# Layer 1 of the last token block as seven multiplications, and the steps around it regrouped

## The chip, the core and the metric

One core of a Trainium2 chip runs the whole kernel. Times are device microseconds (us) of one launch; the time of a kernel is the median of its runs. The engines of the core are TensorE (PE: multiplications, with PEld for the loading of the stationary operand), VectorE (DVE), ScalarE (ACT), GpSimd (POOL) and SyncE (SP, which only issues DMAs here). Each takes its own instructions in the order in which the program wrote them, and waits on semaphores for the others.

## The reference

```python
# q, k, v: (8, 8, 576, 64); a causal window of 64 positions
attn = softmax(where(0 <= rel < 64, q @ k.T / 8, -1e6)) @ v        # (8, 8, 576, 64)
x    = attn.transpose(0, 2, 1, 3).reshape(4608, 512)
h    = maximum(x @ w_in, 0.0)                                       # (4608, 2048): layer 1
out  = (h * h) @ w_out                                              # (4608, 512): layer 2, float32
```

## The kernel before

**Blocks and stages.** The 4608 tokens are nine blocks of 512: blocks 0 to 7 are the first 512 positions of the eight batches, block 8 (`B`, the last) the 64 positions left over in each. The scheduling is by hand (`tc.manual_schedule`): what is written first is issued first on each engine. From `n = 1` to `n = 8` the program goes through stages. Stage `n` lists layer 2 of block `n` (`second`) and layer 1 of block `n + 1` (`first`), merges them by the string `order` (a "1" takes the next step of layer 1, a "2" one of layer 2) into the list `fill`, and hangs everything else (attention of block `n + 2`, sums, loads) on places of that list with `put(i, ...)`. Before item `i` of `fill` the work put at `i` is issued. Stage 7 has layer 2 of block 7 and layer 1 of block 8 and no attention any more; stage 8 has layer 2 of block 8 alone, and then the kernel ends.

**Layer 1 (`F1`, L351).** For one chunk of 128 features: four multiplications of 128x128 by 128x512 into a PSUM bank (`hps`, one of two banks of `ps_f1`), then VectorE takes max(., 0) into `hr` (L361), and ScalarE squares it into `h2` in fp16 (L362). Sixteen such items make a block.

**Layer 2 (`L2S`, L453).** From block 2 on it is done with seven multiplications in place of eight (Strassen's method in Winograd's form): both matrices are cut into 2x2 parts, sums of parts are made beforehand (`S_sum` of h, per half `s` of 128 tokens, into `hsum`; `T_sum` of `w_out`, once, into `wsum`), and the products 1, 2, 6, 5, 7, 3, 4 accumulate in three places: `c` (called chain), and the two halves `pa`, `pb` of another bank (side). One item is eight multiplications of 128x128 by 128x256. Products 6, 7 and 4 go on adding to what stands in `c`, and product 3 to what stands in `pb`; after each product ScalarE (`scaled`, L460) or VectorE (`plus`, L463) takes the state that is wanted to the output tile `osb`. So 14 items make layer 2 of a block. In stage 8 the first half of the tokens uses two extra banks (`more`, from `ps_f1`), so that two halves can alternate.

**Queues.** The ten buffers of pool `stp` (tag "st") stage the loads of q, k, v; the five of `tpool` (tag "T") hold transposed q and k; the four of `apool` (tag "pm") the attention weights. `at_ps` are two PSUM tiles of two banks each, which the attention uses. x of block 8 reaches `xT` by DMA transposes (L336). Output is stored by SP; the last stores go out by SP, POOL and ACT (L490 to L509).

Of the kernel before, what the change touches and what calls it, by code (L numbers as in the profile page):

```python
# [8 lines left out]
FP32 = mybir.dt.float32  # L9
FP16 = mybir.dt.float16  # L10
AF = mybir.ActivationFunctionType
ALU = mybir.AluOpType
# [3 lines left out]
def kernel(  # L16
# [13 lines left out]
    nc = tc.nc  # L30
# [3 lines left out]
    P = 128  # L34
    HP = H // 2
    NBLK = B + 1
    DMC = DM // P
    FFC = DFF // P
# [16 lines left out]
    ps_f1 = ctx.enter_context(tc.tile_pool(name="ps_f1", bufs=2, space=bass.MemoryType.PSUM))  # L55
# [47 lines left out]
    st = {}  # L103
# [12 lines left out]
    def copy(engine, out, in_):  # L116
        if engine is nc.scalar:
            engine.activation(out=out, in_=in_, func=AF.Copy, scale=1.0)  # L118
# [126 lines left out]
    pm, av, xs, xT = {}, {}, {}, {}  # L245
    at_ps = [ps_at.tile([P, 2, 512], FP32, name=f"at{i}") for i in range(2)]
# [84 lines left out]
    def X(g, hp, engine=nc.scalar, pool=ps_tr, tag="tr", own=None):  # L331

        if g not in xT:
            xT[g] = xtpool.tile([P, DMC, 512], FP16, name="xT", tag="xT")
        if g == B:
            nc.sync.dma_start_transpose(out=xT[g][:, hp, :].rearrange("p (j t) -> p j t", j=4),  # L336
                                        in_=xs[g, hp][:].rearrange("p j h d -> p (j h d)"))
            return
        if own is not None:
            tr = at_ps[own][:, 0, :].bitcast(FP16).rearrange("p (a b) -> p a b", a=2)  # L340
        else:
            tr = pool.tile([P, 2, 512], FP16, name="xtr", tag=tag)
        for jp in range(4):
            nc.tensor.transpose(out=tr[:, 0, jp * P:(jp + 1) * P], in_=xs[g, hp][:, jp, :, :],  # L344
                                identity=ident[:])
        copy(engine, xT[g][:, hp, :], tr[:, 0, :])


    h2 = {}

    def F1(g, f, pool=ps_f1, tag="f1", into=None):  # L351
        if g not in h2:
            h2[g] = h2pool.tile([P, FFC, 512], FP16, name="h2", tag="h2")
        hps, done = open_f1.pop((g, f), (None, 0))
        if hps is None:
            hps = into if into is not None else pool.tile([P, 512], FP32, name="hps", tag=tag)
        for c in range(done, DMC):
            nc.tensor.matmul(hps[:], w_in_sb[:, c, f * P:(f + 1) * P], xT[g][:, c, :],  # L358
                             start=(c == 0), stop=(c == DMC - 1))
        hr = opool.tile([P, 512], FP32, name="hr", tag="hr")  # L360
        nc.vector.tensor_scalar(out=hr[:], in0=hps[:], scalar1=0.0, scalar2=None, op0=ALU.max)  # L361
        nc.scalar.activation(out=h2[g][:, f, :], in_=hr[:], func=AF.Square)  # L362
# [41 lines left out]
    HF = FFC // 2  # L404
    HC = DM // 2
# [12 lines left out]
    def s_of(k, s):  # L418
        return S_sb[:, k - 1, :, 128 * s:128 * s + 128]

    def minus(out, a, b, op=ALU.subtract, engine=None):
        (engine or nc.vector).tensor_tensor(out=out, in0=a, in1=b, op=op)  # L422
# [11 lines left out]
    def S_sum(g, k, s):  # L434
        if k == 1:
            minus(s_of(1, s), a_of(g, 1, 0, s), a_of(g, 1, 1, s), ALU.add)
        elif k == 2:
            minus(s_of(2, s), s_of(1, s), a_of(g, 0, 0, s))
        elif k == 3:
            minus(s_of(3, s), a_of(g, 0, 0, s), a_of(g, 1, 0, s))  # L440
        else:
            minus(s_of(4, s), a_of(g, 0, 1, s), s_of(2, s))

    def product(to, a, b, start):
        for f in range(HF):
            nc.tensor.matmul(to, a[:, f, :], b[:, f, :], start=start and f == 0, stop=f == HF - 1,  # L446
                             skip_group_check=True)

    def flush():
        while to_store:  # L450
            to_store.pop(0)()
# [59 lines left out]
    ORDER = (1, 2, 6, 5, 7, 3, 4)  # L511

    seq = list(range(NBLK))
# [3 lines left out]
    with tc.manual_schedule():  # L517
# [21 lines left out]
        dve, pool, act = nc.vector, nc.gpsimd, nc.scalar  # L539
# [60 lines left out]
        three = [in_f1, in_f1, in_f2]  # L600
# [60 lines left out]
        first = iter([lambda f=f: F1(g1, f, into=at_ps[1][:, 1, :] if f == 2 else None) for f in range(FFC)])  # L661
# [5 lines left out]
        def A(g, hp, i=1):  # L667
            AV(g, hp, i)
            N(g, hp)
# [36 lines left out]
        done = 12  # L706
        chain = ps_f2.tile([P, 512], FP32, name="chain", tag="f2")
        side = ps_tr.tile([P, 512], FP32, name="side", tag="tr")
        for n in range(1, NBLK):
            g = seq[n]  # L710
            last = n == NBLK - 1
            one = None if last else seq[n + 1]
            if n == 1:
                second = [lambda ts=ts, i=i: F2(g, ts, i, None, None, into=(chain, side)[ts % 2])
                          for ts in range(4) for i in range(4)]
            elif last:
                more = [ps_f1.tile([P, 512], FP32, name="more", tag="f1") for _ in range(2)]
                banks = [(more[0][:, 0:HC], more[1]), (chain[:, 0:HC], side)]
                second = [lambda p=p, s=s: L2S(g, p, s, banks[s])
                          for p, s in ((1, 0), (2, 0), (1, 1), (6, 0), (2, 1), (5, 0), (7, 0),  # L720
                                       (6, 1), (3, 0), (4, 0), (5, 1), (7, 1), (3, 1), (4, 1))]
            else:
                second = [lambda p=p, s=s: L2S(g, p, s, (chain[:, 0:HC], side))
                          for s in range(2) for p in ORDER]
            first = [] if last else [lambda f=f: F1(one, f) for f in range(FFC)]
            order = ("22222222" + 8 * "112" if n == 1 else
                     "2" * 14 if last else
                     ("2112121212121211" if n == 2 else "1212121212121211") + "21212121121122")
            a, b = iter(first), iter(second)
            fill = [next(a if c == "1" else b) for c in order]  # L730
            at = {}

            def put(i, *work):
                at.setdefault(i, []).extend(work)

            if n == 1:
                put(0, lambda: Sc(g2, 3), lambda: A(g2, 2))
                put(2, lambda: M(g2, 3))
                put(3, lambda: X(g2, 2, own=1))
                put(5, lambda: A(g2, 3))  # L740
                put(7, lambda: X(g2, 3, own=1))
                for i, k in ((1, 1), (3, 2), (6, 3), (8, 4)):
                    put(i, lambda k=k: T_sum(k))
            else:
                for i, k, s in (((0, 1, 1), (0, 2, 1), (2, 4, 0), (3, 3, 1), (4, 4, 1)) if last else
                                ((2, 4, 0), (4, 1, 1), (6, 2, 1), (9, 3, 1), (18, 4, 1))):
                    put(i, lambda k=k, s=s: S_sum(g, k, s))
            if not last:
                end = len(fill) - 1
                put(24 if n == 1 else 20, lambda: S_sum(one, 3, 0))  # L750
                put(end if n == 1 else end - 1, lambda: S_sum(one, 1, 0))
                put(end, lambda: S_sum(one, 2, 0))
            base = 4 * (n + 2)
            for i, two in zip((11, 22) if n == 1 else (9, 20) if n == 2 else (9, 17) if n == 6 else (8, 19),
                              (units[base:base + 2], units[base + 2:base + 4])):
                for t, u in enumerate(two):
                    if u is not None:
                        put(i, lambda u=u, t=t: Sc(*u, i=t))
                        put(i + 3 + t, lambda u=u: M(*u))
                        put(i + 6, lambda u=u, t=t: A(*u, i=t))  # L760
                        put(i + (7 if u[0] == B else 8 + t), lambda u=u, t=t: X(*u, own=t))
            for i, group in enumerate(fill):
# [38 lines left out]
```

## Time and profile before

| what | us |
|---|---|
| median of 3 runs (range) | 298.98 (298.89 to 299.31) |
| the profiled execution | 298.21 |
| its span, first to last instruction | 296.2 |
| stage 7: first matmul of layer 1 of block 8 to first of stage 8 | 253.63 to 279.67 |
| stage 8: to the start of its last matmuls' item | 279.67 to 291.02 |
| last copy of the output on ACT, last DMA issue | 292.11, 292.52 |

Read it so: times in the traces count from the start of the span, and what lies around the span (298.21 - 296.2 = 2.0 us) is launch and end. A group of matmuls in the timeline starts when its first one starts; the next group's start tells when PE was free again, since the ends shown include the way through the array. A duration on ACT or DVE is start to finish of one instruction; the next one may start a little before that end.

### The profile page before, as it was taken

To read this page: it belongs to the slowest core of one execution; us is meant where nothing else is said; L and a number is where in the kernel's file an instruction comes from. 1 tells how busy PE (TensorE), PEld (TensorE's weight loads), DVE (VectorE), ACT (ScalarE), POOL (GpSimd) and SP (SyncE) were. 2 spreads that over 40 slices of the span, in tenths; PEclk is the share of its full clock that TensorE was granted. 3 is DMA by queue.
4 is the path that set the end of the run, shared out by engine and by line. 5 is a ranking of instruction groups with operands and counts; after the bars stand their busy time and mean duration, and the time that the engine had idled before them with its cause. 6 is when DMAs were issued, how large, how long until landed. Compare 5 with 4: busy or idle time off the path is not lost.

```text
span 296.2 us, 7372 instructions
## 1 busy us (share of the span) xinstructions
PE 287.7 (97%) x2905; PEld 180.3 (61%) x2905; DVE 216.3 (73%) x379; ACT 170.3 (57%) x292; POOL 125.8 (42%) x215
## 2 busy tenths in 40 slices
PE   7899999999999999999999999999999999999994
PEld 5543545555445466667666766676667666766783
DVE  4677539588867787878778877987788679866651
ACT  3666757688366656565665566556655654444521
POOL 4668848984383267229425633913232000000002
PEclk9999999999999999999999999999999999999999
DMA  6999999999999995999999999799997023100015
GB/s 209 259 323 392 407 326 237 321 247 196 177 254 185 190 216 106 209 181 234 181 207 226 200 180 226 157 198 200 196 221 202 2 38 107 73 37 35 2 71 142
DMA packets 143650, 56.05 MB, mean 189 GB/s; under 512 B 127712, under 2 KB 136160, under 8 KB 143616
## 3 DMA queue, kind: packets, MB, share of 16 engines
q1 hardware_dynamic: 143232, 55.00, 85.2%
q0 software_dynamic: 144, 0.39, 0.6%
q8 instruction: 22, 0.36, 0.5%
q10 hardware_dynamic: 240, 0.20, 0.3%
q14 instruction: 12, 0.10, 0.1%
HBM read 38.80 MB, written 9.44 MB: 163 GB/s over the span
## 4 chain that ended last, share of the span: by engine, by line
PE 88%; SPq 5%; DMA 4%; POOL 1%; ACT 0%; issue 0%; DVE 0%
PE hps L358 39%; PE chain L446 16%; PE side L446 12%; PE ops L394 5%; DMA wsum<-in_moe_w_in_dram 4%; PE at L318 4%; PE at L288 3%; PE side L394 2%; PE chain L394 2%; SPq L180 2%; PE more L446 2%; PE at L344 2%; SPq L173 2%; PE tr L257 1%; SPq L132 1%; SPq L139 1%
## 5 line engine op out<-in xcount | busy, mean ns | idle before, releaser
L362 ACT ACTIVATE h<-hr 128x512 f16<-128x512 f32 x144 | 90.2, 630 | 92.5 <-DVE hr L361 92.1
L358 PE MATMUL hps<-xT,w_in_sb 128*128 128x512 f16 x560 | 138.6, 379 | 0.5 <-POOL w_in_sb L120 0.4
L361 DVE TENSOR_SCALAR hr<-hps 128x512 f32<-128x512 f32 x143 | 97.2, 687 | 42.6 <-PE hps L358 39.4
L358 PEld LDWEIGHTS <-w_in_sb 128*128 128x128 f16 x564 | 52.8, 98 | 48.1 <-POOL w_in_sb L120 1.9
L446 PEld LDWEIGHTS <-hsum 128*128 128x128 f16 x448 | 43.2, 98 | 13.2
L120 POOL CAST v_ev<-st_v 128x512 f16<-128x512 f32 x31 | 21.6, 696 | 45.3 <-DMA st_v<-in_v_dram 45.3
L446 PEld LDWEIGHTS <-h 128*128 128x128 f16 x336 | 32.7, 98 | 9.3
L120 POOL CAST k<-st_k 128x512 f16<-128x512 f32 x33 | 21.4, 651 | 38.2 <-DMA st_k<-in_k_dram 30.4
L295 ACT ACTIVATE pm<-at 128x1024 f16<-128x1024 f32 x35 | 34.1, 1014 | 2.1 <-PE at L288 2.1
L387 POOL DMA_DIRECT2D out_dram<-osb x3 | 1.8, 595 | 63.6 <-ACT osb L460 62.2
L446 PE MATMUL chain<-wsum,hsum 128*128 128x256 f16 x208 | 27.0, 273 | 0.0
L328 DVE TENSOR_TENSOR xs<-at,rden 128x512 f16<-128x512 f32 x36 | 24.9, 692 | 1.2
L302 DVE TENSOR_TENSOR pm<-pm,mask 128x1024 f16<-128x1024 f16 x32 | 23.7, 754 | 1.9 <-ACT pm L295 1.9
L422 DVE TENSOR_TENSOR hsum<-h 128x1024 f16<-128x1024 f16 x28 | 20.4, 728 | 5.4 <-ACT h L362 5.4
L233 POOL CAST v_od<-st_v 64x512 f16<-64x512 f32 x30 | 22.4, 748 | 1.6
L120 POOL CAST q<-st_q 128x512 f16<-128x512 f32 x28 | 19.2, 711 | 4.7 <-DMA qT<-q 2.1
L394 PEld LDWEIGHTS <-h 128*128 128x128 f16 x128 | 11.6, 98 | 12.2
L460 ACT ACTIVATE osb<-chain 128x256 f32<-128x256 f32 x39 | 14.5, 373 | 5.6 <-PE chain L446 5.6
L318 PEld LDWEIGHTS <-pm 128*64 128x64 f16 x576 | 11.2, 110 | 6.9 <-DVE pm L302 3.2
L118 ACT ACTIVATE xT<-at 128x512 f16<-128x512 f16 x22 | 12.8, 587 | 4.0 <-PE at L344 4.0
L394 PE MATMUL ops<-w_out_sb,h 128*128 128x512 f16 x64 | 14.8, 380 | 0.0
L318 PE MATMUL at<-v_ev,pm 128*64 128x65 f16 x384 | 13.8, 197 | 0.2 <-ACT v_ev L118 0.2
(91 smaller groups left out, 317.2 us busy)
## 6 DMA issues: line engine op xcount, KB each, us to landing
st_k<-in_k_dram SPq DMA_DIRECT2D x37, 256.0 KB, 3.7
out_dram<-osb SPq DMA_DIRECT2D x32, 256.0 KB, 2.8
st_q<-in_q_dram SPq DMA_DIRECT2D x29, 256.0 KB, 4.9
st_v<-in_v_dram SPq DMA_DIRECT2D x28, 256.0 KB, 4.1
w_st<-in_moe_w_in_dram SPq DMA_DIRECT2D x4, 512.0 KB, 5.9
wsum<-in_moe_w_in_dram SPq DMA_DIRECT2D x4, 512.0 KB, 9.8
hsum<-in_moe_w_out_dram SPq DMA_DIRECT2D x4, 512.0 KB, 7.9
wsum<-in_moe_w_out_dram SPq DMA_DIRECT2D x4, 512.0 KB, 9.2
```

Of the source, the lines that this page charges most:

```text
L120: engine.tensor_copy(out=out, in_=in_)
L233: nc.gpsimd.tensor_copy(out=od[g][to:to + 64, m, :, 0:D], in_=st["v", g, c][of:of + 64, :].rearrange("p (h d) -> p h d", h=H))
L295: nc.scalar.activation(out=p[:, hh, :] if apart else p[:], in_=sc[hh] if apart else both[:], func=AF.Exp, scale=1.0 / float(D) ** 0.5)
L302: nc.vector.tensor_tensor(out=p[:], in0=p[:], in1=m.unsqueeze(1).broadcast_to([P, 2, 512]), op=ALU.min)
L318: nc.tensor.matmul(a[jj * 64:(jj + 1) * 64, hh, jp * VW:jp * VW + D + 1], pm[g, hp][:, hh, j * 64:(j + 1) * 64], vsel, start=True, stop=True)
L328: nc.vector.tensor_tensor(out=x[:].rearrange("p j h d -> p h j d"), in0=a[:, :, :, 0:D], in1=rden[:].unsqueeze(3).broadcast_to([P, 2, 4, D ...
L358: nc.tensor.matmul(hps[:], w_in_sb[:, c, f * P:(f + 1) * P], xT[g][:, c, :], start=(c == 0), stop=(c == DMC - 1))
L361: nc.vector.tensor_scalar(out=hr[:], in0=hps[:], scalar1=0.0, scalar2=None, op0=ALU.max)
L362: nc.scalar.activation(out=h2[g][:, f, :], in_=hr[:], func=AF.Square)
L394: nc.tensor.matmul(f2[g, ts][:], h2[g][:, f, ts * P:(ts + 1) * P], w_out_sb[:, f, :], start=(f == 0), stop=(f == FFC - 1))
L422: (engine or nc.vector).tensor_tensor(out=out, in0=a, in1=b, op=op)
L446: nc.tensor.matmul(to, a[:, f, :], b[:, f, :], start=start and f == 0, stop=f == HF - 1, skip_group_check=True)
```

## The change

Layer 1 of block 8 alone is changed from 16 `F1` items to 14 `L1S` items; layers 1 of all other blocks stay. `L1S` cuts `w_in` by 256-deep halves `k` and 1024-feature halves `i`, and x by halves `k` and 256-token halves `j`. `W_sum` makes four sums of parts of `w_in` (each in two VectorE instructions of 128x1024: two in stage 5, four in stage 6, two in stage 7), `X_sum` four sums of parts of x (128x512 each, one in stage 6, three in stage 7). One item is the product `p` for two feature pairs `m`: eight multiplications of 128x128 by 128x256, into one bank per `m`. There are three banks per `m`: `a`, `b` (the `at_ps` tiles, free by then) and `c` (the two of `ps_f1`). Between products ScalarE copies: product 5 to SBUF (`kept5`), 1 from `a` to `b`, 6 from `b` to `c`, 7 from `c` to `a`. VectorE finishes: products 2 and 4 by max(., 0) as before; products 7 and 3 by adding `kept5` (L515 of the changed kernel), and then ScalarE takes max(., 0) for 7 (L518), VectorE max and square in one for 3 (L521). The squares and these last steps are kept in two lists, `later["act"]` and `later["dve"]`, of which one each is issued after every item of `fill` (`catch_up(1, 1)`), and all that is left before stage 8.

Stage 7 (`apart`, where `n == NBLK - 2`) has 28 items instead of 30. In stage 8 the second half's `chain` is moved to a bank of `at_ps[1]`, the order becomes 1, 1, 2, 2, 6, 5, ... (before: 1, 2, 1, 6, 2, 5, ...), and the sums of h for its first half, three of which were made in stage 7, are all made in stage 8. DMAs, their order and their queues stay.

```diff
+    def product1(to, m, a, b, start):
+        for u in range(2):
+            f = (2 * m + u) * P
+            for cc in range(2):
+                nc.tensor.matmul(to[:, u * HX:(u + 1) * HX], a[:, cc, f:f + P], b[:, cc, :],
+                                 start=start and u == 0 and cc == 0, stop=cc == 1, skip_group_check=True)
...
+    def catch_up(d=99, a=99):
+        for engine, n in (("dve", d), ("act", a)):
+            for _ in range(min(n, len(later[engine]))):
+                later[engine].pop(0)()
...
+        def square(m, i, j, hr):
+            later["act"].append(lambda: nc.scalar.activation(out=h_of(m, i, j), in_=wide(hr), func=AF.Square))
+        def done(m, i, j, bank):
+            hr = piece32("ls")
+            nc.vector.tensor_scalar(out=hr[:], in0=bank, scalar1=0.0, scalar2=None, op0=ALU.max)
+            square(m, i, j, hr)
+        def done5(m, i, j, bank, relu_on_act):
+            y = piece32("ls")
+            nc.vector.scalar_tensor_tensor(out=y[:], in0=bank, scalar=1.0, in1=kept5[m][:],
+                                           op0=ALU.mult, op1=ALU.add)
+            if relu_on_act:
+                later["act"].append(lambda: nc.scalar.activation(out=y[:], in_=y[:], func=AF.Relu))
+                square(m, i, j, y)
+            else:
+                later["dve"].append(lambda: nc.vector.scalar_tensor_tensor(
+                    out=h_of(m, i, j), in0=wide(y), scalar=0.0, in1=wide(y), op0=ALU.max, op1=ALU.mult))
...
+        for m in two:
+            product1(banks[m % 2][to], m, lhs, rhs, start)
+        for m in two:
+            a, b, c = banks[m % 2]
+            if p == 5:
+                kept5[m] = piece32("p5")
+                copy(nc.scalar, kept5[m][:], b)
+            elif p == 1:
+                copy(nc.scalar, b, a)
+            elif p == 2:
+                done(m, 0, 0, a)
+            elif p == 6:
+                copy(nc.scalar, c, b)
+            elif p == 7:
+                copy(nc.scalar, a, c)
+                later["dve"].append(lambda m=m, c=c: done5(m, 1, 1, c, m < 2 or RELU[0]))
+            elif p == 3:
+                later["dve"].append(lambda m=m, b=b: done5(m, 0, 1, b, RELU[1]))
+            else:
+                done(m, 1, 0, a)
+    RELU = (True, False)
...
-                banks = [(more[0][:, 0:HC], more[1]), (chain[:, 0:HC], side)]
+                banks = [(more[0][:, 0:HC], more[1]), (at_ps[1][:, 0, 0:HC], side)]
-                          for p, s in ((1, 0), (2, 0), (1, 1), (6, 0), (2, 1), (5, 0), (7, 0),
+                          for p, s in ((1, 0), (1, 1), (2, 0), (2, 1), (6, 0), (5, 0), (7, 0),
...
+            if apart:
+                cs = [ps_f1.tile([P, 512], FP32, name="c", tag="f1") for _ in range(2)]
+                three = [(at_ps[0][:, i, :], at_ps[1][:, i, :], cs[i][:]) for i in range(2)]
+                first = [lambda p=p, two=two: L1S(one, p, two, three)
+                         for two in ((0, 1), (2, 3)) for p in (5, 1, 6, 2, 7, 3, 4)]
+                     "11221121122122" * 2 if apart else
...
+                if last and i == 0:
+                    catch_up()
                 for work in at.pop(i, []):
                     work()
...
                 group()
+                catch_up(1, 1)
```

More of the change, by code (lines that the diff above doesn't have):

```diff
@@ L447, in product, with w_of, x_of, W_sum @@
                              skip_group_check=True)
+    wsums, xsums = {}, {}
+    HX = 256
+    def w_of(i, k):
+        return w_in_sb[:, 2 * k:2 * k + 2, i * HF * P:(i + 1) * HF * P]
+    def x_of(g, k, j):
+        return xT[g][:, 2 * k:2 * k + 2, j * HX:(j + 1) * HX]
+    def W_sum(k, engine, cc):
+        if k not in wsums:
+            t = tpool.tile([P, HP, 512], FP16, name="wS", tag="T")
+            wsums[k] = t[:].rearrange("p a b -> p (a b)").rearrange("p (c f) -> p c f", c=2)
+        a, b, op = {1: (w_of(1, 0), w_of(1, 1), ALU.add), 2: (wsums.get(1), w_of(0, 0), ALU.subtract),
+                    3: (w_of(0, 0), w_of(1, 0), ALU.subtract), 4: (w_of(0, 1), wsums.get(2), ALU.subtract)}[k]
+        cols = slice(cc * 512, cc * 512 + 512)
+        minus(wsums[k][:, :, cols], a[:, :, cols], b[:, :, cols], op, engine)
@@ new lines, in X_sum @@
+    def X_sum(g, k):
+        if k not in xsums:
+            t = apool.tile([P, 2, 512], FP16, name="xS", tag="pm", bufs=4)
+            xsums[k] = t[:, 0, :].rearrange("p (c t) -> p c t", c=2)
+        a, b = {1: (x_of(g, 0, 1), x_of(g, 0, 0)), 2: (x_of(g, 1, 1), xsums.get(1)),
+                3: (x_of(g, 1, 1), x_of(g, 0, 1)), 4: (x_of(g, 1, 0), xsums.get(2))}[k]
+        minus(xsums[k], a, b)
+    def product1(to, m, a, b, start):
[4 more added lines that the diff above has]
+                                 start=start and u == 0 and cc == 0, stop=cc == 1, skip_group_check=True)
@@ new lines, with L1S, h_of, wide @@
+    kept5 = {}
+    later = {"dve": [], "act": []}
+    def catch_up(d=99, a=99):
+        for engine, n in (("dve", d), ("act", a)):
+            for _ in range(min(n, len(later[engine]))):
+                later[engine].pop(0)()
+    def L1S(g, p, two, banks):
+        if g not in h2:
+            h2[g] = h2pool.tile([P, FFC, 512], FP16, name="h2", tag="h2")
+        def h_of(m, i, j):
+            return h2[g][:, i * HF + 2 * m:i * HF + 2 * m + 2, j * HX:(j + 1) * HX]
+        def wide(t):
+            return t[:].rearrange("p (u t) -> p u t", u=2)
+        def piece32(name):
+            return stp.tile([P, 512], FP32, name=name, tag="st")
+        def square(m, i, j, hr):
[14 more added lines that the diff above has]
+                    out=h_of(m, i, j), in0=wide(y), scalar=0.0, in1=wide(y), op0=ALU.max, op1=ALU.mult))
+        to, lhs, rhs, start = {5: (1, wsums.get(1), xsums.get(1), True), 1: (0, w_of(0, 0), x_of(g, 0, 0), True),
+                               2: (0, w_of(0, 1), x_of(g, 1, 0), False), 6: (1, wsums.get(2), xsums.get(2), False),
+                               7: (2, wsums.get(3), xsums.get(3), False), 3: (1, wsums.get(4), x_of(g, 1, 1), False),
+                               4: (0, w_of(1, 1), xsums.get(4), False)}[p]
+        for m in two:
[18 more added lines that the diff above has]
+                done(m, 1, 0, a)
@@ L723 @@
                 second = [lambda p=p, s=s: L2S(g, p, s, (chain[:, 0:HC], side))
-                          for s in range(2) for p in ORDER]
-            first = [] if last else [lambda f=f: F1(one, f) for f in range(FFC)]
+                          for s in range(2) for p in ((1, 2, 6, 5, 7, 3, 4) if n == NBLK - 2 else ORDER)]
+            apart = n == NBLK - 2
+            if apart:
[3 more added lines that the diff above has]
+                         for two in ((0, 1), (2, 3)) for p in (5, 1, 6, 2, 7, 3, 4)]
+            else:
+                first = [] if last else [lambda f=f: F1(one, f) for f in range(FFC)]
             order = ("22222222" + 8 * "112" if n == 1 else
                      "2" * 14 if last else
+                     "11221121122122" * 2 if apart else
                      ("2112121212121211" if n == 2 else "1212121212121211") + "21212121121122")
@@ L749 @@
                 end = len(fill) - 1
-                put(24 if n == 1 else 20, lambda: S_sum(one, 3, 0))
-                put(end if n == 1 else end - 1, lambda: S_sum(one, 1, 0))
-                put(end, lambda: S_sum(one, 2, 0))
+                if not apart:
+                    put(24 if n == 1 else 20, lambda: S_sum(one, 3, 0))
+                if not apart:
+                    put(end if n == 1 else end - 1, lambda: S_sum(one, 1, 0))
+                    put(end, lambda: S_sum(one, 2, 0))
             base = 4 * (n + 2)
```

12 lines of the change are left out of this document (11 added, 1 removed).

## The prediction

> **What bounds the kernel now.** I read the page first, then the chain of waits, then the engines by stage, then single instructions in the timeline.
>
> ```profile
> PE 287.7 (97%) x2905; PEld 180.3 (61%) x2905; DVE 216.3 (73%) x379; ACT 170.3 (57%) x292; POOL 125.8 (42%) x215
> PEclk9999999999999999999999999999999999999999
> L362 ACT ACTIVATE h<-hr 128x512 f16<-128x512 f32 x144 | 90.2, 630 | 92.5 <-DVE hr L361 92.1
> L361 DVE TENSOR_SCALAR hr<-hps 128x512 f32<-128x512 f32 x143 | 97.2, 687 | 42.6 <-PE hps L358 39.4
> ```
>
> PE is busy for 97% at full clock, and ACT and DVE mostly idle for its sake. The chain of waits, in order of time (start, us, what), confirms it to the end:
>
> ```profile
> 261.60 0.87 PE chain L446 x8
> ...
> 265.95 1.73 PE hps L358 x8
> ...
> 279.83 1.75 PE more L446 x16
> ...
> 291.19 0.89 PE chain L446 x8
> ```
>
> Here is the price of an item. Eight multiplications of 256 columns pass in 0.87 us (16 in 1.75: 0.109 each); eight of 512 columns in 1.73, so that an F1 item of four takes 0.865 (0.216 each). Stages 7 and 8, with busy us and counts of each engine:
>
> ```profile
> core 0: us, PE busy (x) PEld busy (x) DVE busy (x) ACT busy (x) POOL busy (x), PEclk, DMA share, GB/s
> ...
> 253.60:279.70 26.10, 26.10 (x179) 17.28 (x178) 18.11 (x31) 12.37 (x24) 0.00 (x0) 1.00 0.11 42
> 279.70:296.20 16.50, 12.36 (x114) 10.83 (x111) 6.97 (x14) 3.46 (x9) 1.78 (x3) 1.00 0.34 95
> ```
>
> Stage 7 has no gap on PE: 16 x 0.865 + 14 x 0.872 = 26.05, and 253.63 to 279.67 is 26.04. POOL does nothing and DMA little. ACT has half of the stage free. For the queues of ACT and DVE I need two numbers of each instruction: when it is done, and when the next may start. The timeline gives both:
>
> ```profile
> 152.66 0.58 ACT L118 ACTIVATE xT<-at 128x512 f16<-128x512 f16 x1
> 153.13 0.38 ACT L460 ACTIVATE osb<-chain 128x256 f32<-128x256 f32 x1
> 153.40 0.60 ACT L118 ACTIVATE xT<-at 128x512 f16<-128x512 f16 x1
> ...
> 231.03 0.69 DVE L361 TENSOR_SCALAR hr<-hps 128x512 f32<-128x512 f32 x1 [0.32 <-PE hps L358]
> 231.76 0.63 ACT L362 ACTIVATE h<-hr 128x512 f16<-128x512 f32 x1 [0.71 <-DVE hr L361]
> 232.29 0.37 ACT L460 ACTIVATE osb<-side 128x256 f32<-128x256 f32 x1
> ...
> 254.15 0.42 DVE L463 SCALAR_TENSOR_TENSOR osb<-side,osb 128x256 f32<-128x256 f32 x1
> 254.49 0.68 DVE L422 TENSOR_TENSOR hsum<-hsum,h 128x1024 f16<-128x1024 f16 x1
> 255.09 0.68 DVE L361 TENSOR_SCALAR hr<-hps 128x512 f32<-128x512 f32 x1
> 255.69 0.68 DVE L422 TENSOR_TENSOR hsum<-h,hsum 128x1024 f16<-128x1024 f16 x1
> ```
>
> ACT: a 128x512 copy out of PSUM is done after 0.59 and the next starts after 0.48; a square from SBUF 0.63 and 0.53; an eviction of 256 columns 0.37 and 0.27. DVE: 0.69 and 0.60 for 128x512 in float32 or 128x1024 in fp16, 0.42 and 0.34 for 256 columns. The hand-over from one engine to the next is 231.76 - 231.72 = 0.04.
>
> **The change part by part.**
>
> *Multiplications.* 16 F1 items (13.84) go, 14 L1S items of 8 x 0.109 = 0.872 come (12.21). All 28 items of the stage need 24.42 against 26.04: **-1.62**, if PE never waits. The operands change, not the form; the loading of weights is 98 ns per 109 ns pass in layer 2 already and shows no gap. The Trainium skill speaks against this (TensorE: Matmul & The Clock Gate, section Back-to-back issue gap): in a stream with weight loads it gives 131 ns for 512 columns and 81 for 128. By that, an estimate between its figures, 98 ns for 256 columns, would make 112 x 0.098 = 11.0 against 64 x 0.131 = 8.4, a loss of 2.6 us. The trace disagrees (0.216 and 0.109 above), so that outcome gets less than 0.01.
>
> *Work on ACT.* The 16 squares become 12 squares and 4 relus, all from SBUF, and 16 copies of 128x512 are new, 12 of them from PSUM to PSUM. In start-to-start times: 16 x 0.53 + 16 x 0.48 + 8 evictions x 0.27 = 18.3 us in a stage of 24.4 (before 10.6 in 26.0). It fits, but in-order: the question is when each copy lets PE go on.
>
> *Work on DVE in the stage.* Out: 16 relus and three sums of h. In: 8 relus, 8 additions of kept5, 4 relu-squares, three sums of x, two of w_in: 20 x 0.60 + 3 x 0.34 + 2 x 0.60 = 14.2 for 19 x 0.60 = 11.4. The additions and relu-squares have no row at 512 columns. Their own form takes 0.42 at 256 (L463), so they lie between 0.68 (the 128x1024 fp16 row, whose 512 steps of two are as many) and 0.84 (twice 0.42); L361 has their size and type, so 0.69.
>
> *Sums ahead of the stage.* Six sums of w_in and one of x, 6 x 0.60 + 0.34 = 3.9 us on DVE in stages 5 and 6, where DVE is idle for about 6 us in 30. An F1 item's bank is wanted again two F1 items later, 1.73 after its end at the tightest; the way through the array (the timeline shows 1.03 for an item of 0.865), hand-over and relu take 0.16 + 0.04 + 0.69 of it, which leaves 0.84 for one sum of 0.60 in front. I cost them at nothing; without that cover each would cost up to 0.60, 3.6 in all. x of block 8 is there: before, all four chunks are read from 253.63 on without a gap.
>
> *The walk through stage 7.* I take ACT's and DVE's queues in the changed order, each instruction at the later of its engine's free time and its inputs plus 0.04 (0.07 more where the late input is waited for by a separate instruction), and PE's items every 0.872. The copy inside PSUM has no row; I take the 0.59 of the copy out of PSUM. Gate by gate:
> - Product 6 of the first pairs (257.12) wants product 1 copied into `b`: product 5 is copied 254.76 to 255.83, then product 1 at 255.87 and, behind it because both write one tile, at 256.50, done 257.09. Just in time.
> - Product 7's copies (261.19 to 262.41) release DVE's additions (261.88, 262.51), whose relu (262.61) and square (263.27) stand on ACT in front of layer 2's eviction of side, done 264.18. PE's next item into side could start at 264.10 and starts at 264.21: **+0.11**.
> - The squares of product 4 hold ACT until 267.0, so that product 5 of the second pairs is copied from 267.28 and product 1 only until 269.61. Product 6 wants it at 269.45: **+0.19**. The same place in side costs nothing this time (276.62, when its eviction has just been done).
> - Stage 8 starts at 278.37 (before 279.67). What is late next is the sums of h: the last relu-square on DVE is done 280.39, two sums in a row 281.17 and 281.88, and product 6 wanted them at 281.86; with the weight load after the wait it starts 281.98: **+0.11**. Behind DVE's sums only `plus` waits, which has slack. The second half's chain in its own bank is free from 277.6 and used at 279.24. Sums for later products have 0.4 us and more.
>
> The same walk over the old order gives the old trace: no wait, stage 8 at 279.67. The order of stage 8's last items and stores is unchanged, so the 4.1 us from the last matmul to 296.2 stay.
>
> Sum: -1.62 + 0.11 + 0.19 + 0.11 = **-1.21** with copies of 0.59. Reading PSUM in place of SBUF takes ACT from 0.63 to 0.59; if writing it spares the same 0.04 the three waits shrink to 0.27, **-1.35**. I take the middle, -1.3. On the profiled execution that is a span of 294.9 and 296.9 in all; on the median, 298.98 - 1.3 = **297.7**.
>
> Bounds of the copy: 0.37, the eviction of 256 columns, and 1.01, the 128x1024 row. The walk with them gives -1.62 (from 0.49 down every gate is open) and +2.1; at 0.69 it gives -0.6, at 0.79 0.0, at 0.99 +1.8. With additions of 0.84 it gives -0.3, with 0.68 -1.26.
>
> **The rivals.**
> - *All hidden*: copies into PSUM at 0.49 or less, no gate late: -1.62, **297.4**. For: PSUM is the quicker side for ACT's reads in these rows. Against: no row of a write. The Trainium skill (ScalarE: Activation LUTs, section Step-by-step: what each stage is for) says that ScalarE writes PSUM with lower latency than SBUF, which leads here; no trace shows it yet.
> - *The gain goes into waits*: copies at 0.7 to 0.79, or hand-overs of 0.065 in place of 0.04 (then -0.5): -0.6 to 0, **298.7**. The items would be fewer, but PE would stand at the two product 6 gates and at side for as long. Against: hand-overs are 0.03 to 0.04 in every idle ACT or DVE row.
> - *Slower: ACT becomes the bound of stage 7.* Place: ACT's queue from 254.8 to 279; price: at 0.99 a copy ACT has 16 x 0.53 + 4 x 0.48 + 12 x 0.88 + 2.2 = 23.2 us of 24.4, each product 6 and 4 waits 0.6 to 1.0, in all +1.8: **300.8**. It decides from a copy of 0.79 on. For: nothing in the trace writes PSUM from ACT. Against: ACT's times go by columns (0.37, 0.59, 1.01 for 256, 512, 1024), whatever the type.
> - *DVE late*: one sum in two holds a relu up by its uncovered 0.1 to 0.2 in stages 5 and 6 (0.3 to 0.6), or additions at 0.84 (-0.3), both together: about 0, **299.0**. For: DVE is the busier engine there (24 of 30 us).
>
> **How the numbers follow.** Forecast 0.50, all hidden 0.22, waits 0.15, ACT bound 0.06, DVE late 0.07. A measurement of this kernel can tell 0.2% (0.6 us) from no change. Faster by more: 0.50 + 0.22 + 0.04 of the others = 0.76; within: 0.11 + 0.03 = 0.14; slower: 0.06 + 0.04 = 0.10. The range takes in full hiding less 0.2 for the scatter of medians (runs spread 0.4), 297.2, and the copy of 0.69 plus 0.3, 298.7; that leaves out the slower cases and half of the waits.
>
> **What would show it.** Stage 7 of the changed kernel should last 24.7 us from its first product 5 to stage 8's first item; the copies at -> at should have a mean near 0.55 to 0.59; waits of PE on ACT should stand at side and at the second product 6, 0.1 to 0.2 each, and one on DVE's sums in stage 8; stages 2 to 6 should keep their length. A copy above 0.75, or gaps of 0.5 at product 6, would prove it wrong, and so would any wait of hps on DVE in stages 5 and 6.

## The result and the profile after

| | us |
|---|---|
| before, median of 18 runs (range) | 298.39 (297.0 to 300.95) |
| changed, median of 18 runs (range) | 297.62 (295.84 to 298.29) |
| ratio of changed to before, 95% interval | 0.9958 (0.9938 to 0.9978) |
| in us of 298.39 | -1.25 (-1.85 to -0.66) |
| profiled execution of the changed kernel, its span | 298.29, 296.6 |

By the ratio the kernel is faster by 1.25 us, against 1.3 forecast. The ratio is close to that of the means of the runs, 298.64 and 297.38; the two medians lie only 0.77 apart. The interval keeps clear of no change, but the size is known no better than that. Yet the profiled execution has a longer span than before (296.6 for 296.2). The two are reconciled by cutting each span where the program passes a fixed place (us, each row from one profile):

| stretch | before | changed | difference |
|---|---|---|---|
| start to the first `L2S` matmul of block 2 | 105.60 | 107.14 | +1.54 |
| from there to stage 7 | 148.03 | 148.13 | +0.10 |
| stage 7 | 26.04 | 24.70 | -1.34 |
| stage 8, first matmul to last | 12.12 | 12.16 | +0.04 |
| last matmul to the end | 4.44 | 4.44 | 0 |

The head, which the change doesn't touch, took 1.54 us longer in this one execution. More on it below. First the page's row of engines, and those of layer 1's relus and squares, of the changed kernel:

```profile
PE 287.0 (97%) x2953; PEld 185.0 (62%) x2953; DVE 225.5 (76%) x395; ACT 178.1 (60%) x308; POOL 126.7 (43%) x215
L362 ACT ACTIVATE h<-hr 128x512 f16<-128x512 f32 x128 | 80.1, 630 | 80.0 <-DVE hr L361 79.6
L361 DVE TENSOR_SCALAR hr<-hps 128x512 f32<-128x512 f32 x127 | 85.8, 686 | 31.3 <-PE hps L358 28.2
```

PE has 48 matmuls more in the records, but they are shorter ones: its busy time fell by 0.7 us. ACT and DVE took on 7.8 and 9.2 us, and 16 of the old squares are gone (144 to 128). Busy us and counts of each engine in stages 7 and 8:

```profile
core 0: us, PE busy (x) PEld busy (x) DVE busy (x) ACT busy (x) POOL busy (x), PEclk, DMA share, GB/s
255.27:279.97 24.70, 24.70 (x227) 21.91 (x225) 19.53 (x36) 19.49 (x39) 0.00 (x0) 1.00 0.12 44
279.97:296.60 16.63, 12.43 (x114) 10.72 (x111) 9.30 (x18) 4.32 (x11) 1.78 (x3) 1.00 0.34 96
```

The clock is full (1.00), as before. ACT went from 12.37 us in 26.10 to 19.49 in 24.70, so it isn't full, and PE shows as busy all the time. The short waits stand in the chain of waits (start, us, what), as pieces longer than their 0.87 for eight:

```profile
265.92 0.97 PE side L446 x8
...
271.25 1.89 PE at L480 x16
...
283.62 2.67 PE more L446 x24
```

0.97 is 0.10 too long for eight, 1.89 0.15 for sixteen (1.74), 2.67 0.05 for 24 (2.62). PE's timeline has the first matmuls behind these waits:

```profile
265.85 1.03 PE L446 MATMUL side<-w_out_sb,hsum 128*128 128x256 f16 x8
...
271.24 1.03 PE L480 MATMUL at<-xS,wS 128*128 128x256 f16 x8
...
283.50 0.72 PE L446 MATMUL more<-wsum,hsum 128*128 128x256 f16 x5
```

The items ahead of them started at 264.88, 270.21 and 282.59, so with 0.872 for an item the waits are 0.10, 0.16 and 0.04. What each waited for stands in the timelines of ACT and DVE of the changed kernel (in brackets, where there is one, the idle time before the instruction and who ended it):

```profile
264.89 0.63 ACT L506 ACTIVATE h<-ls 128x512 f16<-128x512 f32 x1
265.43 0.37 ACT L562 ACTIVATE osb<-side 128x256 f32<-128x256 f32 x1
...
268.88 1.08 ACT L118 ACTIVATE p<-at 128x512 f32<-128x512 f32 x2
269.99 1.20 ACT L118 ACTIVATE at<-at 128x512 f32<-128x512 f32 x2
```

```profile
281.24 0.68 DVE L521 SCALAR_TENSOR_TENSOR h<-ls 128x512 f16<-128x512 f32 x1
282.02 0.69 DVE L422 TENSOR_TENSOR hsum<-h 128x1024 f16<-128x1024 f16 x1
282.75 0.69 DVE L422 TENSOR_TENSOR hsum<-hsum,h 128x1024 f16<-128x1024 f16 x1
```

The eviction of side is done at 265.80 and PE starts at 265.85. The pair of copies of product 1 is done at 271.19 and PE starts at 271.24. The second sum of h is done at 283.44 and PE starts at 283.50. These are the three places that the forecast named. The groups of stages 7 and 8, for the prices (behind the bar: busy us, mean ns of one; then the idle time before):

```profile
L515 DVE SCALAR_TENSOR_TENSOR ls<-at,p 128x512 f32<-128x512 f32 x4 | 2.7, 680 | 0.0
L521 DVE SCALAR_TENSOR_TENSOR h<-ls 128x512 f16<-128x512 f32 x4 | 2.7, 680 | 0.0
...
L518 ACT ACTIVATE ls<-ls 128x512 f32<-128x512 f32 x4 | 2.5, 625 | 0.4 <-DVE ls L515 0.2
L118 ACT ACTIVATE at<-c 128x512 f32<-128x512 f32 x4 | 2.3, 585 | 0.1
...
L118 ACT ACTIVATE p<-at 128x512 f32<-128x512 f32 x4 | 2.2, 596 | 0.5 <-PE at L480 0.5
L118 ACT ACTIVATE c<-at 128x512 f32<-128x512 f32 x4 | 2.1, 580 | 1.8 <-PE at L480 1.8
```

A copy from PSUM to PSUM takes 0.580 to 0.585, one from PSUM to SBUF (`p`) 0.596. DVE's additions and relu-squares take 0.68, as L361 does.

### The profile page after: what moved, and what is told of

Read it like the earlier page. It is cut to its first block, busy times and chain, and to the rows that moved or that the text cites. A ratio compares the mean times of both kernels' runs of the same rounds, so it can differ in the third digit from the quotient of the medians.

```text
span 296.6 us, 7511 instructions
## 1 busy us (share of the span) xinstructions
PE 287.0 (97%) x2953; PEld 185.0 (62%) x2953; DVE 225.5 (76%) x395; ACT 178.1 (60%) x308; POOL 126.7 (43%) x215
## 4 chain that ended last, share of the span: by engine, by line
PE 88%; SPq 6%; DMA 4%; POOL 1%; ACT 0%; issue 0%; DVE 0%
PE hps L358 34%; PE chain L446 14%; PE side L446 12%; PE ops L394 5%; PE at L480 4%; PE at L318 4%; DMA wsum<-in_moe_w_in_dram 4%; PE at L288 3%; PE side L394 2%; PE chain L394 2%; SPq L180 2%; PE more L446 2%; SPq L173 2%; PE at L344 2%; PE at L446 1%; PE tr L257 1%
## 5 line engine op out<-in xcount | busy, mean ns | idle before, releaser
L362 ACT ACTIVATE h<-hr 128x512 f16<-128x512 f32 x128 | 80.1, 630 | 80.0 <-DVE hr L361 79.6
L358 PE MATMUL hps<-xT,w_in_sb 128*128 128x512 f16 x496 | 122.7, 379 | 0.6 <-POOL w_in_sb L120 0.4
L361 DVE TENSOR_SCALAR hr<-hps 128x512 f32<-128x512 f32 x127 | 85.8, 686 | 31.3 <-PE hps L358 28.2
L358 PEld LDWEIGHTS <-w_in_sb 128*128 128x128 f16 x500 | 46.7, 98 | 43.2 <-issue 1.4
L120 POOL CAST v_ev<-st_v 128x512 f16<-128x512 f32 x31 | 22.3, 720 | 43.6 <-DMA st_v<-in_v_dram 43.6
L422 DVE TENSOR_TENSOR hsum<-h 128x1024 f16<-128x1024 f16 x28 | 21.6, 770 | 5.2 <-ACT h L362 5.1
L446 PE MATMUL chain<-wsum,hsum 128*128 128x256 f16 x192 | 24.9, 273 | 0.0
L318 PEld LDWEIGHTS <-pm 128*64 128x64 f16 x576 | 11.2, 110 | 6.9 <-DVE pm L302 3.0
L318 PE MATMUL at<-v_ev,pm 128*64 128x65 f16 x384 | 13.7, 198 | 0.2 <-ACT v_ev L118 0.2
L562 ACT ACTIVATE osb<-chain 128x256 f32<-128x256 f32 x36 | 13.4, 372 | 0.3 <-PE chain L446 0.3
```

The costliest lines, as they stand in the source:

```text
L318: nc.tensor.matmul(a[jj * 64:(jj + 1) * 64, hh, jp * VW:jp * VW + D + 1], pm[g, hp][:, hh, j * 64:(j + 1) * 64], vsel, start=True, stop=True)
```

## The experiments

The theory: PE's 28 items set stage 7, and only three gates in front of PE cost time, by the order in which ACT and DVE reach the work that opens them; outside stages 7 and 8 the change costs nothing. The rivals: the gain lies elsewhere, the gates are not what the waits hang on, or the new sums cost time in the stages before.

**Both kernels once more**, unchanged, in 12 further runs each.

> The kernel before, unchanged, against itself, for what a run of it scatters by. The head theory (the whole time scatters by when the first loads of q, k, v and w_in land, before 30 us, and the stages after that always take the same): ratio 1.000 within its interval, runs spread over 2 us or more, stage 7 in the profile 26.04 us from its first matmul to stage 8's, stage 8's items 12.4, and the profile's span differs from 296.2 by what PE is early or late at the first layer 1 item of block 0. The rival (the stages themselves scatter): stage 7 differs from 26.04 by 0.2 or more.

> The changed kernel once more. The gates theory (PE's items plus what ACT's queue holds up): stage 7 again 24.70 us from its first product 5 to stage 8's first item, with the two waits of 0.10 and 0.16 at the same items, whatever the head does; ratio to the kernel before 0.9955 to 0.9965 (-1.05 to -1.35 us). The rival (the gain of 18 runs was partly luck of the heads): ratio above 0.998.

Measured: before 298.35 (297.08 to 299.9), ratio to its own other runs 1.0013 (0.9989 to 1.0037), stage 7 26.04. Changed 297.2 (296.13 to 298.3), ratio 0.9959 (0.9936 to 0.9982), stage 7 24.69. Stage 7 returns to 0.01 us, the whole times scatter by 2 to 3 us. The stretch ahead of stage 7 took 147.91 before and 148.36 after.

**The sums alone.** The kernel before, with the seven-product scheme's sums of `w_in` and x put at the changed kernel's places; no multiplication reads them. The lines below call `W_sum` and `X_sum` as the change has them.

```diff
+            for i, k, cc in {NBLK - 4: ((19, 1, 0), (22, 1, 1)),
+                             NBLK - 3: ((2, 2, 0), (9, 2, 1), (17, 3, 0), (26, 3, 1)),
+                             NBLK - 2: ((3, 4, 0), (17, 4, 1))}.get(n, ()):
+                put(i, lambda k=k, cc=cc: W_sum(k, dve, cc))
+            if n == NBLK - 3:
+                put(25, lambda: X_sum(seq[-1], 1))
+            if n == NBLK - 2:
+                for i, k in ((0, 2), (2, 3), (4, 4)):
+                    put(i, lambda k=k: X_sum(one, k))
```

> The kernel before with the sums of w_in and x of the changed kernel added on DVE at their places in stages 5, 6 and 7; their results are not used. If DVE covers them, as forecast: no wait of PE in stages 5 to 7, stage 7 26.04 us, stages 5 and 6 as long as before within 0.05 us. If DVE is late there (the rival): waits of hps on DVE in stages 5 and 6, 0.2 to 0.6 us in all.

Measured: one run of 298.77. Stage 7 26.04 and stage 8 12.12, as before; from block 2 to stage 7 it took 148.40, against 148.03 and 147.91 in the two profiles of the kernel before. So the sums do cost time in stages 5 and 6, about 0.4 us, and the theory fell on this point. The list of waits names no wait of PE from 110 to 254 us in either kernel: the loss is seen only from start to start. DVE's timeline of this kernel at the place where the two part, and then PE's:

```profile
217.53 0.68 DVE L302 TENSOR_TENSOR pm<-pm,mask 128x1024 f16<-128x1024 f16 x1
218.13 1.10 DVE L422 TENSOR_TENSOR wS<-w_in_sb 128x1024 f16<-128x1024 f16 x1
219.15 0.68 DVE L302 TENSOR_TENSOR pm<-pm,mask 128x1024 f16<-128x1024 f16 x1
219.75 1.27 DVE L361 TENSOR_SCALAR hr<-hps 128x512 f32<-128x512 f32 x2
220.95 0.19 DVE L325 RECIPROCAL rden<-at 128x8 f32<-128x8 f32 x1
```

```profile
225.07 1.15 PE L358 MATMUL hps<-xT,w_in_sb 128*128 128x512 f16 x4
226.11 1.03 PE L446 MATMUL chain<-w_out_sb,h 128*128 128x256 f16 x8
```

The same two views of the kernel before:

```profile
217.44 1.70 DVE L302 TENSOR_TENSOR pm<-pm,mask 128x1024 f16<-128x1024 f16 x2
219.06 1.28 DVE L361 TENSOR_SCALAR hr<-hps 128x512 f32<-128x512 f32 x2
220.25 0.19 DVE L325 RECIPROCAL rden<-at 128x8 f32<-128x8 f32 x1
```

```profile
224.76 1.03 PE L358 MATMUL hps<-xT,w_in_sb 128*128 128x512 f16 x4
225.62 1.04 PE L446 MATMUL chain<-w_out_sb,h 128*128 128x256 f16 x8
```

One sum stands between the two minimums of the attention's mask (`pm`). The second minimum starts at 219.15, and the reciprocal (`rden`) at 220.95 in place of 220.25. Behind it come the division, the transposes on PE and the copies of `xT` on ACT, and the first F1 item of stage 6 reads that `xT`: its successor starts 1.04 after it (226.11 - 225.07), where before it was 0.86 (225.62 - 224.76). That is 0.18. The rest of the loss lies earlier, at the second half of the attention's multiplications (L318), which read the second `pm`: the layer 2 item behind them starts 2.66 after the F1 items at 217.60, where before it was 2.45 after those at 217.50. Over the whole place PE is later by 226.11 - 225.62 = 0.49, of which 0.10 was there before it (an F1 item at 217.60 in the one and 217.50 in the other): 0.39.

**No lists.** All that stands in the two lists is issued after each item, so that relus and squares run as early as they can.

```diff
-                catch_up(1, 1)
+                catch_up()
```

> The changed kernel with everything in the two lists issued at once behind its product, not one per item. Gates theory: DVE's additions for product 7 then stand right behind it, where they wait for ACT's copies, and the squares and relus stand on ACT in front of the next copies and evictions: PE waits 1.36 and 1.24 us, once in each half; stage 7 27.05 us in place of 24.70. The rival (ACT has a quarter of the stage free, the order in its queue matters little): stage 7 24.7 to 25.0.

Measured: stage 7 27.03, one run 298.52. The waits of PE from 230 us to the end (us in total, times, longest), of this kernel:

```profile
PE side L446 <- ACT osb L562: 2.3, 2, 1.2
```

and the part of its chain of waits that leads there:

```profile
261.53 0.70 DVE ls L515
...
262.26 0.64 ACT ls L518
...
262.92 0.63 ACT h L506
263.55 0.53 ACT ls L518
...
264.64 0.38 ACT osb L562
```

ACT has to wait for DVE's addition, and takes a relu, a square, a relu and a square of product 7 before the eviction of side. This is the first gate. From start to start, as above, the item in `side` waits 265.06 - 262.82 - 0.872 = 1.37 in place of 0.10, and once more in the second half 1.23, against 1.36 and 1.24 forecast (the list of waits counts from the modelled end of the item before, hence 1.20 and 1.06). With the products but without the lists, stage 7 would be 1.0 longer than before the change (27.03 - 26.04).

**One copy more in front of the second gate.** The copy of product 1 is made twice for each pair.

```diff
             elif p == 1:
                 copy(nc.scalar, b, a)
+                copy(nc.scalar, b, a)
```

> The changed kernel with the copy of product 1 from bank a to bank b made twice, that is four more copies of 0.58 inside PSUM on ACT. Gates theory: product 6 waits for the last of them, 1.22 us in the first half and 1.41 in the second (before 0 and 0.16); stage 7 27.16 us. The rival (ACT's spare time takes four more copies, 2.3 us of 6): stage 7 24.7 to 25.3.

Measured: stage 7 27.14, one run 299.3. Its waits of PE from 230 us on:

```profile
PE at L480 <- ACT at L118: 2.3, 2, 1.2
```

and the chain ahead of the first of them:

```profile
256.04 0.59 ACT at L118
...
256.65 0.59 ACT at L118
...
257.88 0.59 ACT at L118
```

Four copies more make the stage 2.44 longer, 0.61 each. That is one copy and 0.02 or 0.03 up to the next: these copies, which write one tile, don't overlap (the chain's starts are 0.61 apart; why, is in the last section), and all of it reaches PE. From start to start product 6 waits 1.22 and 1.38, against 1.22 and 1.41 forecast. In the first half the gate had been just in time, as forecast, in the second it was 0.16 late.

**Stage 8 in the old order and the old bank.**

```diff
-                banks = [(more[0][:, 0:HC], more[1]), (at_ps[1][:, 0, 0:HC], side)]
+                banks = [(more[0][:, 0:HC], more[1]), (chain[:, 0:HC], side)]
-                          for p, s in ((1, 0), (1, 1), (2, 0), (2, 1), (6, 0), (5, 0), (7, 0),
+                          for p, s in ((1, 0), (2, 0), (1, 1), (6, 0), (2, 1), (5, 0), (7, 0),
```

> The changed kernel with the order of stage 8's items and the bank of its second half's chain as before (1, 2, 1, 6, 2, 5, ...); the sums of h stay all in stage 8. Gates theory: product 6 of the first half stands one item earlier, but the sums of h that it needs are ready at the same time as before, some 3.5 us into the stage: PE waits about 0.9; stage 7 24.70, stage 8 13.03 from its first to its last matmul in place of 12.16. The rival (the regrouping of stage 8 is neutral): 12.1 to 12.3.

Measured: stage 8 13.04 (12.16 in the changed kernel), one run 298.43; stage 7 24.69. Its waits of PE from 280 us on:

```profile
PE more L446 <- DVE hsum L422: 0.7, 1, 0.7
```

In the old order product 6 comes one item earlier and has to wait for the sums of h, which are now all made in stage 8, for 0.91 us (282.78 - 281.00 - 0.872; the list of waits counts 0.74, from the modelled end of the item before). In the changed kernel it waits 0.04. The edit puts back the order and the bank, but no other wait of PE stands in this stage, so the order is what is worth 13.04 - 12.16 = 0.88. It pays for the sums that were moved out of stage 7.

**The list of ACT held back.** It is not served after items 8, 11 to 14 and 22, which stand in front of the first two gates, and two are issued after items 16 and 17 to make up for it.

```diff
-                catch_up(1, 1)
+                catch_up(1, {8: 0, 11: 0, 12: 0, 13: 0, 14: 0, 16: 2, 17: 2, 22: 0}.get(i, 1) if apart else 1)
```

> The changed kernel with ACT's list held: no square or relu from it after items 8, 11 to 14 and 22 of stage 7, two after items 16 and 17. Gates theory: the eviction of side then stands before the square, the copies of product 5 and 1 before the squares of product 4, and PE waits nowhere: stage 7 28 x 0.873 = 24.44 us, 0.26 less than 24.70; stage 8 no later than before; ratio to the kernel before 0.9945 to 0.9955. The rival (the 0.26 us that PE waits come from PE or from the hand-over itself, not from the order in ACT's queue): stage 7 stays at 24.65 to 24.75.

Measured: stage 7 24.45, stage 8 12.12, median 296.92 (296.13 to 297.58, 12 runs), ratio 0.994 (0.992 to 0.996), a little under the 0.9945 forecast. The products and their copies are the same; with other places for the squares all three gates are open in time: 28 x 0.872 = 24.42. From block 2 to stage 7 it took 148.42.

**The same, and one sum moved.** The second sum of stage 5, the one between the two minimums, goes from place 22 to place 28.

```diff
-            for i, k, cc in {NBLK - 4: ((19, 1, 0), (22, 1, 1)),
+            for i, k, cc in {NBLK - 4: ((19, 1, 0), (28, 1, 1)),
```

> The kernel with ACT's list held, and the second part of the first sum of w_in moved from item 22 to item 28 of stage 5. New theory for stages 2 to 6 (that one sum, put in front of the second minimum with the mask, makes DVE late for the attention: first the second pair's matmuls with v wait about 0.2, then two relus, their squares and the copy to xT are late, and the first layer 1 item of stage 6 waits 0.2): from the first layer 2 item of block 2 to stage 7 147.9 to 148.05 us as in the kernel before, in place of 148.1 to 148.4; stage 7 24.45, stage 8 12.12; ratio to the kernel before 0.993 to 0.995. The rival (all seven sums ahead of the stage cost a little each, or the longer code does): still 148.3 or more.

Measured: from block 2 to stage 7 147.91, stage 7 24.45, stage 8 12.12; median 296.64 (295.48 to 297.89, 12 runs), ratio 0.9954 (0.9929 to 0.9979), a little over the 0.995 forecast. The timeline of all its engines has, at the two places:

```profile
217.57 1.28 DVE L302 TENSOR_TENSOR pm<-pm,mask 128x1024 f16<-128x1024 f16 x2
...
224.89 1.03 PE L358 MATMUL hps<-xT,w_in_sb 128*128 128x512 f16 x4
...
225.75 1.04 PE L446 MATMUL chain<-w_out_sb,h 128*128 128x256 f16 x8
```

The two minimums stand together again, and the F1 item takes 0.86 (225.75 - 224.89). In the seven profiles of kernels with the sum at place 22 this stretch takes 148.13 to 148.45, 148.34 in the mean; in the three without it or with it moved 147.91 to 148.03, 147.95 in the mean. Moving one of the seven sums takes back all of it: 148.42 in the kernel with the list held, 147.91 here, and nothing else was changed between these two. By its stages this kernel is 1.6 us ahead of before (24.45 - 26.04 = -1.59) and beats both. Between it and the changed kernel the whole times can't decide: the two ratios and their intervals are almost the same.

The ten profiles say more about this place. Count from the start of the two F1 items beside the minimums (217.60 in the kernel with the sums alone). In the seven profiles with the sum there, the second minimum is done at 2.05 to 2.34, and the `chain` item of the views (226.11 there) starts 6.28 to 6.29 after that, at 8.34 to 8.62. In the three others the minimum is done at 1.22 to 1.63, and the item starts at 8.12 all the same. So the minimum has room until about 8.12 - 6.28 = 1.84. The sum's 0.60 on top of 1.22 just fits into that; the 0.23 to 0.52 beyond it don't, and in all seven a cast on POOL makes one or two of the three instructions that much longer (1.10 in place of 0.68 in the kernel with the sums alone; more in the last section). That the sum alone would be free is an estimate from these numbers: no profile has it there without a cast beside one of the three.

## Why the prediction was right, and where it failed

- *The multiplications*: right. Stage 7 was forecast at 24.7 and took 24.70. In the kernel with open gates it takes 24.45, of which 24.42 are 28 items at 0.872. The outcome by the Trainium skill (TensorE: Matmul & The Clock Gate, section Back-to-back issue gap), 2.6 us slower, did not come: layer 1 in items of 256 columns passes at 0.109 per multiplication here.
- *The walk through stage 7*: right in its places, and nearly in size. +0.11 at side was 0.10, +0.19 at the second product 6 was 0.16, and the first product 6 was just in time. The two edits of the lists and the doubled copy moved just these gates, with the engine and the line that the walk names. One reading beside it was too wide: hand-overs are not "0.03 to 0.04 in every idle ACT or DVE row", since the square at 255.86 of the profile before starts 0.09 after its relu is done (255.09 + 0.68). The walk itself allows for such places with its 0.07 more, so nothing in the sum hung on it.
- *Stage 8*: the place was right, the size smaller: 0.04 for 0.11. Counted from the start of the stage, product 6 began 3.53 after it (283.50 - 279.97), where the walk had 3.61 (281.98 - 278.37).
- *The copy in PSUM*: 0.58, close to the 0.59 taken, far from the 0.49 that *all hidden* needed and from the 0.79 of *ACT becomes the bound*. ACT was busy for 19.49 of 24.70. *All hidden* would have been the right outcome with other places for the squares (24.45), not with faster copies.
- *DVE's additions*: 0.68, close to the 0.69 taken, not 0.84.
- *The sums ahead of the stage*: this step failed. "I cost them at nothing", the prediction said, with 0.84 us of slack in the F1 bank as cover for a sum of 0.60. The relus were not what it held up. The step looked at one consumer of DVE and left out the attention, whose minimum of the mask leads, by multiplications, reciprocal, division, transposes and a copy, to the first layer 1 item of the next stage. It also took every sum and minimum at 0.60 from start to start, where one that meets a cast on POOL takes up to 0.45 more (1.13 in place of 0.68 in the kernel with the old stage 8). Together they cost 0.39 to 0.50 in six of the seven profiles and 0.22 in the other, the changed kernel's first, and only one of the sums did so. The rival *DVE late* had the engine and the size (0.3 to 0.6), but another path.
- *The median and the range*: this step failed too. "298.98 - 1.3 = 297.7" stands on three runs, and "0.2 for the scatter of medians (runs spread 0.4)" on the same three. In 18 runs the kernel before has a median of 298.39 and a spread of 4 us, and in two later sets 298.30 (29 runs) and 298.15 (17 runs). By the ratio measured beside it, the time is 298.39 x 0.9958 = 297.1, just under the range's lower end of 297.2. The saving, 1.25, was forecast at 1.3; what was off is the time that it was taken from, by 0.6, and a scatter taken for 0.2. The plain median, 297.62, lies next to the 297.7 by luck: a start that was 0.59 too high met two medians that are 0.77 apart and not 1.3.

In the change itself the sums took 0.1 to 0.4 back, and the waits took 0.30 in place of 0.41. The stages come to -1.20 in the first pair of profiles (-1.34 + 0.04 + 0.10) and to -0.86 in the second (-1.35 + 0.04 + 0.45); both lie in the measured interval of -1.85 to -0.66. So that 1.25 came so close to 1.3 is luck in part as well: the stages gave less, and in the later set a part of the difference is no stage's (next paragraph).

*Where the scatter comes from.* In ten profiles of eight kernels the start of block 2's layer 2 lies between 104.91 and 107.14 us, and no later stretch of one kernel differs by over 0.3. So what scatters inside the span comes from the head, which is the same in all of them. A second part lies outside the span. Where single runs are on record with their spans, a run of the kernel before takes 1.67 to 3.30 us more than its span (over 1.9 in 16 of 57 runs), and one of the changed kernel or of the two with ACT's list held 1.67 to 1.78 (54 runs). In the later set the spans differ by 0.87 in the mean (296.41 and 295.54), close to the -0.86 of the stages, and another 0.17 lies outside (1.89 and 1.72). Why some runs of the kernel before take longer there stays open.

In the head, these are waits of PE before 40 us, in the profile of before:

```profile
PE hps L358 <- POOL w_in_sb L120: 0.4, 2, 0.2
...
PE tr L257 <- DVE q L120: 0.2, 1, 0.2
```

of the changed kernel:

```profile
PE tr L257 <- DVE q L120: 0.8, 2, 0.6
...
PE hps L374 <- POOL w_in_sb L120: 0.4, 1, 0.4
```

PE waits for the first casts of q and `w_in`, 0.6 and 0.4 more than before, together 1.0 of the 1.54. They read what the first loads bring; which load is late, and why, was only read from the rows and not tried, so it stays open.

## What to carry to other kernels

When instructions are put into an engine's idle time, ask of each instruction behind them who waits for it, not only of the one that is tightest in the same stage: here the attention's minimum was on a chain to the next stage's first matmul, and its slack of some 0.6 was partly taken by a cast on another engine. Where copies replace matmuls, the order of the queue that makes them decides the gain: the same products gave 27.03, 24.70 and 24.45 in stage 7 by the places of squares and relus alone. And a saving of 1 us in 300 is read from stages between fixed places (stages 7 and 8 returned to 0.01, the stretch before them to 0.2), rather than from whole times that scatter by 3 us; a range needs that scatter from more than three runs.

## What the hardware did that I had not expected

- *A sum on DVE and a cast on POOL hold each other up.* POOL's timeline of the kernel with the sums alone:

```profile
217.84 0.85 POOL L120 CAST v_ev<-st_v 128x512 f16<-128x512 f32 x1 [0.89 <-DMA st_v<-in_v_dram]
```

The sum at 218.13, with two operands in SBUF, took 1.10 in place of 0.68; 0.56 of it lay beside the cast (to 218.69). Before, the second minimum of the pair shown above, from 218.04 on, took as long (the pair lasts 1.70), with 0.55 beside a cast that lasted to 218.59. The same sum without a cast beside it takes 0.68, in the first profile of the changed kernel:

```profile
219.70 0.68 DVE L422 TENSOR_TENSOR wS<-w_in_sb 128x1024 f16<-128x1024 f16 x1
```

And where a minimum was already running when the cast came, in the kernel with the moved sum, the two minimums took 1.28 and the cast 1.16 in place of 0.61:

```profile
218.16 1.16 POOL L120 CAST v_ev<-st_v 128x512 f16<-128x512 f32 x1 [1.18 <-DMA st_v<-in_v_dram]
```

So in these rows the one that came second was longer: the sum and the minimum by 0.42, the cast by 0.55. The Trainium skill (SBUF — State Buffer, section SBUF: two separate sides) says that VectorE with two SBUF inputs and GpSimd lock each other out of a port they share. These rows agree with it; no edit here took the cast away.
- *Writing PSUM spares ACT little.* 0.58 for a copy into PSUM and 0.596 into SBUF, both from PSUM. The Trainium skill (ScalarE: Activation LUTs, section Step-by-step: what each stage is for) has the direction right; the size here is 0.01 to 0.02 us.
- *Copies that write one tile in PSUM follow one another without overlap*: in the chain of the doubled copy they start 0.61 apart, 0.02 after the end of the one before, where copies to other places started 0.48 apart, before the end of the last (the 0.59 and 0.48 of the prediction). This is the program's doing, as far as the trace tells: there each of these copies waits on the semaphore that ACT's own instructions raise when they are done. The two copies of product 6, which write two tiles of their own (`c`), start 0.49 apart, and the second has no such wait. That two tiles in place of one would bring product 1's second copy forward by 0.13 follows from this, but no run tried it.
